# New instruction orders for four engines, and two constants written by GpSimd, in a fused attention and gMLP kernel

## The chip, the cores and the metric

The kernel runs on one core of a Trainium2 chip. The metric is the device time of one execution in microseconds (us); the figure for a kernel is the median of its runs. The engines are called by the names of the profile: PE is TensorE (matmuls), PEld is its weight load, DVE is VectorE, ACT is ScalarE, POOL is GpSimd, SP is SyncE, which here issues most DMAs.

## The reference

Tokens S = 2048, width D = 448, 16 heads of 28, gMLP half width Fh = 896, all bf16. Each token attends to itself and to the 7 tokens at distances 2, 4, ... 14 before it.

```python
# A: sliding, dilated attention on layernorm(x)
qkv = layernorm(x) @ wqkv                      # 16 heads, Dh = 28
idx = pos[:, None] - 2 * arange(8)[None, :]    # mask idx >= 0
attn = softmax(einsum(q, k[idx]) * Dh ** -0.5)
h = x + einsum(attn, v[idx]) @ wo
# B: gMLP on layernorm(h)
z = gelu(layernorm(h) @ w_in)                  # S x 1792
z1, z2 = z[:, :896], layernorm(z[:, 896:])
g = w_sp @ z2 + b_sp[:, None]                  # S x S times S x 896
h2 = h + (z1 * g) @ w_out
```

## The kernel before

The work is cut into 677 tasks, each of one engine, each with a name. A function adds them with the tasks they depend on and the buffers they take and free. The order in which each engine issues its tasks is written out by hand: `SEQ` holds five lists of task numbers, for SP, GpSimd, VectorE, ScalarE and TensorE. A planner (`Planner.replay`) goes through the lists at build time with estimated durations, picks buffers for each task (the eight PSUM banks above all, mostly in pairs), and calls the tasks' emit functions. From the order of emission `Sched` works out which semaphore each instruction waits for. So the lists, and the banks that the planner picks along them, are all that decides the order; nothing is decided at run time.

The stages, with the task names that follow later and their lines in the profile:

- Start: 16 x blocks of 128 tokens are loaded (`x`), and the weights. `c_...` tasks write constants: `c_warm` (128x512 ones, line 614), `c_wo0` (zeros in the padded output weights, 128x896 float32, line 627), `c_wkp` and `c_wqp` (625), `c_V` (628), `c_ident` (618), `c_nhalf` (616). `f0` (635) is 15 matmuls on `warm` that nobody reads; they run before the first real work.
- Layer norm 1, by units of two blocks: `bn1` (statistics, 656 and 657), `rs1` (one over the deviation, on GpSimd at 646 and 647 or on ScalarE at 668 and 669), `nrm1` (676), and a transpose into `xh`, either by a transposing DMA from SP (`tD1`, 683) or on TensorE (`tT1`, 692, with a copy `ev1`).
- Projections: `cpq` and `cpk` copy weights into a padded layout (`cpq100` is the part for one half of the heads). `mmq`, `mmk` (783) and `mmv` (823) are matmuls into a pair of banks, `evq`, `evk` and `evv` copy the banks out, on ScalarE (641) or VectorE (643). `mmk0` needs the units 0 to 3 of `xh`.
- Attention, in 9 blocks of 114 queries, from the last to the first: `mml` (logits, 858), `exp` (870), `mask` (877), `mmr` (sums over keys, 8 matmuls, 886), `ln` and `rex` (899 and 921, the inverse of the sums on ScalarE), `mmo` (values, 911), `ot` (product, 929). Then `mmy` (output projection, 964) and `h` (add to x, 972). `cpw` copies halves of `w_in`.
- Layer norm 2 (`bn2`, `rs2`, `nrm2`, `tD2`), like the first.
- gelu stage: `mmz2` (984) and `mmz1` (1028), groups of 14 matmuls into a pair of banks, emptied by `ge` (994) and `gz1` (1038) on ScalarE; layer norm 3 on the second half (`bn3` at 1000, `ag3` at 1006, `rs3`, `nrm3` at 1014).
- Gating: `g` (1064) multiplies with `w_sp`, 16 matmuls a group, 28 groups; `ua` and `um` (1073) add the bias and multiply. Then `wo` (1093), `oa` (1103) and the stores. `w_sp` arrives by transposing DMAs (`wsp`, 946), each issued when one before it has landed.

An engine issues strictly in list order: if a task waits, all that stands behind it in that list waits too. A task that takes banks waits until the task that empties them has ended.

Of the kernel before, what the change touches and what calls it, by code (L numbers as in the profile page):

```python
# [6 lines left out]
D = 448  # L7
# [21 lines left out]
F32 = mybir.dt.float32  # L29
# [191 lines left out]
class Planner:  # L221
# [12 lines left out]
    def add(self, *a, **k):  # L234
        t = Task(*a, **k)
        self.tasks.append(t)
        self.named[t.name] = t
        return t
# [140 lines left out]
def bass_sequential_preLN__sliding_local_dilated__mixer_gmlp__prompt_kernel(  # L379
# [18 lines left out]
    with contextlib.ExitStack() as top:  # L398
        def sb(name, shape, dt):
            return top.enter_context(nc.sbuf_tensor(name, shape, dt))  # L400
# [14 lines left out]
        reg3 = sb("reg3", [128, n3], BF16)  # L415
# [5 lines left out]
        warm = sb("warm", [128, 512], BF16)  # L421
# [51 lines left out]
        r_wo = [Res("wo%d" % h) for h in range(4)]  # L473
# [20 lines left out]
        r_warm = Res("warm")  # L494
# [113 lines left out]
        def cst(name, fns, dur, eng="pool", deps=()):  # L608
            def em():
                for fn, rd, wr in fns:  # L610
                    iss(eng, fn, reads=rd, writes=wr)
            return add(name, eng, dur, em, deps=deps)

        c_warm = cst("c_warm", [(lambda e: e.memset(warm[:], 1.0), [], [r_warm])], 0.5, eng="dve")
        c_eps = cst("c_eps", [(lambda e: e.memset(epst[:], EPS), [], [r_eps])], 0.1)
        c_nhalf = cst("c_nhalf", [(lambda e: e.memset(nhalf[:], -0.5), [], [r_nhalf])], 0.1)
        c_ident = cst("c_ident", [
# [6 lines left out]
        for p in "kq":  # L624
            c_wp[p] = cst("c_w%sp" % p, [(lambda e, t=wpd[p]: e.memset(t.rearrange("p c (h d) -> p (c h) d", d=32)[:, :, DH:32], 0.0),
                                          [], r_w[p][0] + r_w[p][1])], 0.5)
        c_wo0 = cst("c_wo0", [(lambda e: e.memset(reg3[:, 0:4 * D].bitcast(F32), 0.0), [], r_wo)], 1.0, eng="dve")
        c_V = cst("c_V", [(lambda e, v=v: e.memset(V[:, v, :, :, DH:32], 0.0), [], [r_V[v]]) for v in range(NV)], 0.75)

        def fill(name, n, deps=()):  # L630
# [134 lines left out]
        for ch in range(NCH - 1, -1, -1):  # L765
            for isq in (0, 1):
# [6 lines left out]
                for g0 in range(0, 4, per):  # L773
# [33 lines left out]
                   eng="dve", deps=t_k[NCH - 1] + [c_kpad])  # L807
# [356 lines left out]
```

## Time and profile before

| | us |
|---|---|
| median of 3 runs | 242.24 (242.14 to 242.91) |
| profiled execution | 242.4 |
| its span | 240.7 |
| TensorE busy | 232.7 (97%) |
| VectorE busy | 141.2 (59%) |
| ScalarE busy | 93.6 (39%) |
| GpSimd busy | 26.2 (11%) |

The profile is one execution, seen by instructions. "Busy" leaves out waits and DMA issues. The span runs from the first to the last instruction, and the execution's own time is 1.7 us longer. TensorE works through projections and attention until about 80 us, through the gelu stage until about 119 us, and through gating and output after that.

In the rows of the timeline the columns are start, duration, engine, line, operation, output and input, shape and count; a bracket holds the idle time of that engine just before and what ended it. In the DMA view, queue 8 ("instruction") carries packets of program code.

### The profile page before, as it was taken

To read this page: it belongs to the slowest core of one execution; us is meant where nothing else is said; L and a number is where in the kernel's file an instruction comes from. 1 tells how busy PE (TensorE), PEld (TensorE's weight loads), DVE (VectorE), ACT (ScalarE), POOL (GpSimd) and SP (SyncE) were. 2 spreads that over 40 slices of the span, in tenths; PEclk is the share of its full clock that TensorE was granted. 3 is DMA by queue.
4 is the path that set the end of the run, shared out by engine and by line. 5 is a ranking of instruction groups with operands and counts; after the bars stand their busy time and mean duration, and the time that the engine had idled before them with its cause. 6 is when DMAs were issued, how large, how long until landed. Compare 5 with 4: busy or idle time off the path is not lost.

```text
span 240.7 us, 6694 instructions
## 1 busy us (share of the span) xinstructions
PE 232.7 (97%) x3009; PEld 119.7 (50%) x3019; DVE 141.2 (59%) x281; ACT 93.6 (39%) x112; POOL 26.2 (11%) x66
## 2 busy tenths in 40 slices
PE   7899999999999999999999999999999999999994
PEld 2587755455545444444444444444444444444452
DVE  6999957588998999788800040271201454654443
ACT  2997988888999557664710000000000000000000
POOL 4062000002023313106400000000000000000000
PEclk9999999999999999999999999999999999999999
DMA  7924699331224378979346333200000000010122
GB/s 213 337 51 101 125 146 209 81 71 36 41 41 87 82 116 221 138 168 133 87 87 134 87 87 87 46 0 0 0 0 3 0 0 19 22 59 1 56 76 78
DMA packets 54629, 20.01 MB, mean 83 GB/s; under 512 B 46792, under 2 KB 54472, under 8 KB 54600
## 3 DMA queue, kind: packets, MB, share of 16 engines
q1 hardware_dynamic: 53416, 18.61, 36.0%
q10 hardware_dynamic: 1184, 0.98, 1.5%
q8 instruction: 23, 0.38, 0.6%
q14 instruction: 6, 0.05, 0.1%
HBM read 6.37 MB, written 1.84 MB: 34 GB/s over the span
## 4 chain that ended last, share of the span: by engine, by line
PE 88%; DVE 5%; ACT 1%; issue 1%; DMA 1%; POOL 1%
PE psum L1064 40%; PE psum L783 11%; PE psum L1093 9%; PE psum L984 8%; PE psum L964 5%; PE psum L823 5%; PE psum L1028 4%; PE psum L858 2%; PE psum L911 2%; DVE z2p L1014 2%; DMA x_tm<-in_A_x_dram 1%; PE psum L886 1%; DVE st L1000 1%; DVE st L656 1%; POOL rs L647 1%
## 5 line engine op out<-in xcount | busy, mean ns | idle before, releaser
L1073 DVE TENSOR_TENSOR ub<-psum,reg 128x512 bf16<-128x512 f32 x28 | 18.9, 687 | 68.7 <-PE psum L1064 66.4
L1064 PE MATMUL psum<-reg,z2p 128*128 128x512 bf16 x220 | 49.4, 379 | 0.2
L1064 PE MATMUL psum<-wspT_lo,z2p 128*128 128x512 bf16 x218 | 48.5, 379 | 0.4 <-DVE z2p L1014 0.2
L1064 PEld LDWEIGHTS psum<-wspT_lo,z2p 128*128 128x128 bf16 x224 | 21.8, 98 | 26.6 <-issue 0.4
L1064 PEld LDWEIGHTS psum<-reg,z2p 128*128 128x128 bf16 x224 | 21.9, 98 | 26.2
L783 PE MATMUL psum<-xh,reg 64*128 64x128 bf16 (+2 forms) x448 | 26.1, 270 | 0.1
L1093 PE MATMUL psum<-reg 128*128 128x448 bf16 (+2 forms) x119 | 22.2, 341 | 0.1
L984 PE MATMUL psum<-w_in,xh 64*128 64x448 bf16 x224 | 22.2, 349 | 0.0
L1028 PE MATMUL psum<-xh,w_in 64*128 64x512 bf16 x196 | 21.8, 376 | 0.0
L641 ACT ACTIVATE reg<-psum 128x896 bf16<-128x896 f32 (+2 forms) x25 | 19.9, 847 | 2.2 <-PE psum L823 1.2
L783 PEld LDWEIGHTS psum<-xh,reg 64*128 64x128 bf16 x448 | 16.7, 94 | 7.8 <-issue 0.6
L656 DVE BATCH_NORM_STATS2 st<-x_tm 128x6 f32<-128x448 bf16 x32 | 19.6, 611 | 1.0 <-DMA x_tm<-in_A_x_dram 0.9
L1000 DVE BATCH_NORM_STATS2 st<-z2p 128x6 f32<-128x448 bf16 x32 | 17.5, 610 | 3.6 <-ACT z2p L994 3.6
L870 ACT ACTIVATE reg<-psum 128x928 bf16<-128x928 f32 x18 | 16.2, 939 | 3.0 <-PE psum L858 3.0
L994 ACT ACTIVATE z2p<-psum 128x896 bf16<-128x896 f32 x16 | 14.2, 916 | 7.9 <-PE psum L984 7.9
L1038 ACT ACTIVATE reg<-psum 128x1024 bf16<-128x1024 f32 x14 | 13.6, 1029 | 8.0 <-PE psum L1028 8.0
L1093 PEld LDWEIGHTS psum<-reg 128*128 128x128 bf16 x119 | 11.4, 98 | 10.4
L646 POOL TENSOR_SCALAR rs<-mv 128x2 f32<-128x2 f32 x19 | 6.6, 347 | 87.9 <-DVE mv L657 69.1
L1103 DVE TENSOR_TENSOR tring<-psum,x_tm 128x448 bf16<-128x448 f32 (+2 forms) x17 | 10.1, 596 | 10.2 <-PE psum L1093 10.1
L984 PEld LDWEIGHTS psum<-w_in,xh 64*128 64x128 bf16 x224 | 10.6, 94 | 10.4 <-issue 0.4
L1028 PEld LDWEIGHTS psum<-xh,w_in 64*128 64x128 bf16 x196 | 9.4, 94 | 11.5 <-issue 0.2
L647 POOL TENSOR_TENSOR rs<-rs,nhalf 128x2 f32<-128x2 f32 x19 | 14.6, 770 | 1.6
(62 smaller groups left out, 200.7 us busy)
## 6 DMA issues: line engine op xcount, KB each, us to landing
x_tm<-in_A_x_dram SPq DMA_DIRECT2D x15, 112.0 KB, 4.0
out_dram<-tring SPq DMA_DIRECT2D x15, 112.0 KB, 1.7
w_in<-in_B_w_in_dram SPq DMA_DIRECT2D x2, 448.0 KB, 4.0
reg<-in_B_w_out_dram SPq DMA_DIRECT2D x1, 784.0 KB, 5.2
z2p<-in_A_wqkv_dram ACTq DMA_DIRECT2D x2, 336.0 KB, 4.3
reg<-in_B_b_sp_dram SPq DMA_DIRECT2D x1, 512.0 KB, 4.8
w_in<-in_B_w_in_dram SPq DMA_DIRECT2D x2, 224.0 KB, 3.4
reg<-in_A_wo_dram SPq DMA_DIRECT2D x4, 98.0 KB
```

The lines of the kernel that those rows point to most:

```text
L641: iss("act", lambda e: e.activation(dst, src, AF.Copy), reads=rd, writes=wr)
L647: iss("pool", lambda e: e.tensor_tensor(dst, dst, nh, ALU.pow), reads=rr + [r_nhalf], writes=rr)
L656: iss("dve", lambda e: e.bn_stats(st[:, b, :], x_tm[:, b, :]), reads=[r_x[b]], writes=[rl[b]])
L783: iss("pe", lambda e, c=c, s=s, gi=gi, lhs=lhs: e.matmul(psum[:, bk[s] * 512 + cw * gi:bk[s] * 512 + cw * gi + cw], lhs, xh[64 * s:64 * s ...
L870: iss("act", lambda e: e.activation(E[:, es[0], 2 * n:2 * n + 2, :], pair_view(lb, 0, 8 * JW), AF.Exp, scale=SCALE), reads=[r_bank[lb[0]], ...
L984: iss("pe", lambda e, k2=k2, c=BLK[s][k2], s=s: e.matmul(psum[:, zb[s] * 512:zb[s] * 512 + D], xh[64 * s:64 * s + 64, c, HX + 128 * u:HX + ...
L994: iss("act", lambda e: e.activation(z2p[:, u:u + 9:8, D * k:D * k + D], pair_view(zb, 0, D), AF.Gelu_apprx_tanh), reads=[r_bank[zb[0]], r_ ...
L1000: iss("dve", lambda e, b=b: e.bn_stats(st3[:, b, k, :], z2p[:, b, D * k:D * k + D]), reads=[r_z2[b][k]], writes=[r_st3[b][k]])
L1028: iss("pe", lambda e, k=k, c=BLK[s][k], s=s: e.matmul(psum[:, bk[s] * 512:bk[s] * 512 + 512], w_in[64 * s:64 * s + 64, k, 128 * f:128 * f ...
L1064: iss("pe", lambda e, b=b: e.matmul(psum[:, gb[0] * 512:gb[0] * 512 + 512], z2p[:, b, 128 * f:128 * f + 128], src[:, b, 512 * (tc % 2):512 ...
L1073: iss("dve", lambda e: e.tensor_tensor(ub[:, us_[0], :], psum[:, gb[0] * 512:gb[0] * 512 + 512], bb[:, 512 * tc:512 * tc + 512], ALU.add), ...
L1093: iss("pe", lambda e, f=f: e.matmul(psum[:, wb[0] * 512 + d0:wb[0] * 512 + d1], z1p[f][:, 128 * m:128 * m + 128], w_out[:, f, d0:d1], star ...
```

## The change

No task is added, removed or resized. Two constants change engine, and the lists of GpSimd, VectorE, ScalarE and TensorE are new; SP's list is the same. From the second gating task on (TensorE) and from `ua1_4` on (VectorE) the orders agree with those before, except that `g0_4_0` and `g1_1_0` swap.

What moves, by names:

- GpSimd: `c_warm` first, then `c_wqp`, `c_ident`, `c_wkp`, `c_V`, `c_eps`, `c_xpad`, `c_nhalf`, `c_wo0`; `c_mband` behind `rs1_5` and `c_kpad`; `rs2_0` ahead of `rs3_7`, `rs3_3` ahead of `rs3_4`.
- VectorE: no longer `c_warm` and `c_wo0`; `cpq100` from behind `nrm1_12` to right behind `cpv0`; `mask7` ahead of `nrm1_3`; `evq0_2` leaves for ScalarE, `evq0_3` (ahead of `ot5`) and `evk0_3` (behind `cpw1_0`, ahead of `h7`) come from there; `cpw1_0` behind `cpw1_1`; `nrm2_15` ahead of `h5`, `h2` ahead of `nrm2_5`; `bn3_7_0` ahead of `nrm2_2`, and many small moves among `bn3`, `ag3` and `nrm3`, whose last is now `nrm3_3` instead of `nrm3_1`.
- ScalarE: `cpk001`, `evq3_0`, `evv8` ahead of `cpq101`; `evk3_2` ahead of `cpq110`; `exp8_0` ahead of `exp7_0`; `rs1_2` ahead of `evv6`; `evq1_0` ahead of `exp7_1`; `exp5_0` ahead of `exp6_0`; `evq0_2` behind `exp6_0`; `ln5` ahead of `evk0_1`; `gz1_1_4` ahead of `ge6_1`; `ge6_0` from behind `ge6_1` to behind `ge3_1`; `ge1_1` ahead of `gz1_0_6`, and a few more.
- TensorE: `mmk3_0` two places earlier; `mml6_00` and `mml6_11` one place earlier; `mmr5` ahead of `mmq0_3`; `mmr6` ahead of `mmo5_1`; `mmo3_3` ahead of `mmr2`; some `mmz1` groups earlier among the `mmz2` groups; `g0_4_0` ahead of `g1_1_0`.

```diff
 SEQ = (
     ...
-    (28, 31, 26, 24, 29, 27, 25, 55, 87, 48, 85, 73, 86, 330, 384, 366, 348, 402, 420, 438, 341, 456, 395, 359, 413, 467,
-     431, 377, 449),
+    (23, 29, 26, 28, 31, 24, 27, 25, 30, 55, 48, 85, 87, 73, 86, 330, 384, 366, 348, 402, 420, 438, 456, 341, 413, 395, 359,
+     467, 431, 377, 449),
     ...
-        c_warm = cst("c_warm", [(lambda e: e.memset(warm[:], 1.0), [], [r_warm])], 0.5, eng="dve")
+        c_warm = cst("c_warm", [(lambda e: e.memset(warm[:], 1.0), [], [r_warm])], 0.5)
     ...
-        c_wo0 = cst("c_wo0", [(lambda e: e.memset(reg3[:, 0:4 * D].bitcast(F32), 0.0), [], r_wo)], 1.0, eng="dve")
+        c_wo0 = cst("c_wo0", [(lambda e: e.memset(reg3[:, 0:4 * D].bitcast(F32), 0.0), [], r_wo)], 1.0)
```

The list shown is GpSimd's; the other three are changed in the same way, and `cst` without an engine means GpSimd.

34 rows, old and new, of the table SEQ are left out of this document.

## The prediction

> **What bounds the kernel now.** I read the page first, then the chain of waits in order of time, then the timeline wherever TensorE shows a gap, and the DMA view in narrow windows around those gaps. "PE" is TensorE, "SP" is SyncE.
>
> ```profile
> span 240.7 us, 6694 instructions
> PE 232.7 (97%) x3009; PEld 119.7 (50%) x3019; DVE 141.2 (59%) x281; ACT 93.6 (39%) x112; POOL 26.2 (11%) x66
> PE 88%; DVE 5%; ACT 1%; issue 1%; DMA 1%; POOL 1%
> ```
>
> The first row is the span, the second the busy shares, the third the chain that ended last. TensorE is busy for 97% and carries 88% of the chain. The change removes no matmul, so it can only win where TensorE stands still, and from the gating groups at 119 us to the end TensorE's list is the same but for two neighbouring groups that swap. So I look for TensorE's gaps before 119 us. There are four that matter.
>
> ```profile
> 7.43 0.56 PE L692 MATMUL psum<-ident,tring 128*128 128x128 bf16 x7 [0.33 <-DVE tring L676]
> 17.21 1.59 PEld L783 LDWEIGHTS psum<-xh,reg 64*128 64x128 bf16 x56 [0.18 <-DVE reg L643]
> 50.41 0.70 PE L858 MATMUL psum<-reg 32*64 32x58 bf16 x64
> 51.68 1.52 PE L823 MATMUL psum<-reg,xh 64*64 64x448 bf16 x28 [0.56 <-issue]
> 71.69 1.69 PE L964 MATMUL psum<-reg 128*128 128x448 bf16 x8 [0.58 <-DVE mv L657]
> ```
>
> The bracket is idle time and its releaser. The first gap is the start-up chain; the second waits for a weight copy on VectorE; the third has no releaser ("issue"); the fourth names VectorE, but the VectorE step it names (layer-norm statistics) is none that these matmuls read. Gaps three and four, at 51 and 71 us, I read as the arrival of code for TensorE:
>
> ```profile
> q8 instruction: 23, 0.38, 0.6%
> GB/s 0 0 410 0 0 0 0 0 0 0 0 0 0 0 0 0 0 0 0 0 0 0 0 0 0 0 0 0 0 0 0 0 0 0 0 0 0 0 0 0
> q8 instruction: 1, 0.02, 5.8%
> q8 instruction: 1, 0.02, 5.6%
> 46.75 0.93 ACT L899 ACTIVATE reg<-psum 128x928 f32<-128x928 f32 x1
> 67.98 0.39 PE L886 MATMUL psum<-reg,ones 64*32 64x464 bf16 x8
> ```
>
> Queue 8 brings 23 packets of 0.38 MB / 23 = 16 KB. The GB/s row and the row under it are the DMA view of 48.7 to 50.3 us: one packet, in the third of 40 slices, so at 48.8 us. The third q8 row is 69.0 to 70.1 us: one packet, near 69.1. Both come about 1.1 us after an event that let TensorE's instruction stream go on: `ln6` on ScalarE ended at 46.75 + 0.93 = 47.7 and freed the banks of `mmy7`; `mmr1` began at 67.98. TensorE went on 2.9 us (51.68) and 2.6 us (71.69) after the packet. So where a bank wait holds the stream, the next 16 KB are asked for late, and TensorE stops some 4 us later. The gap at 51 us costs 0.56 idle by its row, and 0.06 more, since a group can start that much ahead of the modelled end of the one before it (60.44 against 60.11 + 0.39, below): some 0.62 us.
>
> **The change part by part.**
>
> Constants. GpSimd starts its own work at 0.78, VectorE at 0.96:
>
> ```profile
> 0.78 0.47 POOL L625 MEMSET reg<- 128x448 bf16 x1 [0.29 <-POOLq L1149]
> 0.96 0.48 DVE L614 MEMSET warm<- 128x512 bf16 x1 [0.96 <-PEq L1149]
> 2.10 0.20 POOL L618 MEMSET ident<- 128x128 bf16 x1
> 3.81 0.10 POOL L616 MEMSET nhalf<- 128x2 f32 x1
> 6.20 0.36 DVE L676 TENSOR_SCALAR tring<-x_tm,mv,rs 128x448 bf16<-128x448 bf16 x1
> 9.66 0.85 SPq L936 DMA_DIRECT2D reg<-in_A_wo_dram  x2
> ```
>
> GpSimd took 0.20 us for 128 elements and 0.47 for 448, so 0.83 ns an element: `c_warm` (512) about 0.53 us, `c_wo0` (896) about 0.85 by elements, up to 1.7 if its 4-byte elements count twice. The warm-up matmuls start some 0.15 us earlier. That buys nothing: what follows them waits until 7.43 for the layer-norm chain, whose list on VectorE is unchanged. GpSimd's list ended at 3.91; with both it ends near 5.5 (6.3 at the upper end) and its first user, the output-weight loads, is issued at 9.66. Cover is ample: cost 0. VectorE gains nothing either, it was waiting for the first x rows. A rule speaks against this part: the Trainium skill, SBUF — State Buffer, in its opening part on the two sides, says that VectorE's two-port modes and GpSimd lock a port pair from each other for a whole instruction. By that rule a late `c_wo0` could hold up the step at 6.20; at 0.85 us it is over by then, and no row here shows such a hold.
>
> The copies at 9 to 17 us. `cpq100` leaves the place that made the 0.18 us wait. But ScalarE now takes a bank copy (`evk3_2`, 0.5 to 0.6 us) ahead of `cpq110`, which the same matmuls need:
>
> ```profile
> 15.54 0.95 ACT L641 ACTIVATE reg<-z2p 64x896 bf16<-64x896 bf16 x1
> ```
>
> `cpq110` ended at 16.49; with 0.6 more it ends near 17.1, and `mmq3_2` starts at about 17.17 instead of 17.21. I take 0, with 0.2 of gain as the other end.
>
> Layer-norm 1, 20 to 33 us. ScalarE's `rs1_2` moves ahead of `evv6`, `exp8_0` ahead of `exp7_0`:
>
> ```profile
> 22.15 0.59 DVE L656 BATCH_NORM_STATS2 st<-x_tm 128x6 f32<-128x448 bf16 x1
> 22.70 0.29 ACT L668 ACTIVATE rs<-mv,epst 128x2 f32<-128x2 f32 x1
> 23.13 0.28 ACT L668 ACTIVATE rs<-mv,epst 128x2 f32<-128x2 f32 x1
> 23.61 0.98 DVE L676 TENSOR_SCALAR tring<-x_tm,mv,rs 128x448 bf16<-128x448 bf16 x3
> 28.42 1.22 SPq L683 DMA_TRANSPOSE xh<-tring  x1
> xh<-tring SPq DMA_TRANSPOSE x1, 4.6
> 33.17 0.60 PE L783 MATMUL psum<-xh,reg 64*128 64x512 bf16 x4
> ```
>
> `rs1_2` must wait for statistics that end as the 22.15 row begins, near 22.2, and behind it stand `evv6` and `rs1_0`. `rs1_0` then starts near 23.5 instead of 23.13, so `nrm1_0`, the second of the three at 23.61, slips by about 0.16 us, and with it VectorE's list up to `nrm1_11` and the transposed loads on SP. The last of these, issued at 28.42, took 4.6 us to land: 33.02, and `mmk0_0`, its user, began at 33.17. No slack: cost 0.15 (from 0 to 0.25).
>
> 35 to 50 us. `evq0_2` goes to ScalarE, `evq0_3` and `evk0_3` to VectorE (1.22 us each, as its cast of that shape at 29.35), `ln5` ahead of `evk0_1`, and `mmr5` ahead of `mmq0_3`. TensorE then leaves its projection matmuls for 8 column-sum matmuls and comes back:
>
> ```profile
> 29.35 1.22 DVE L643 CAST reg<-psum 128x1024 bf16<-128x1024 f32 x1
> 60.11 0.39 PE L886 MATMUL psum<-reg,ones 64*32 64x464 bf16 x8
> 60.44 1.69 PE L964 MATMUL psum<-reg 128*128 128x448 bf16 x8
> 42.47 1.02 ACT L641 ACTIVATE reg<-psum 128x1024 bf16<-128x1024 f32 x1 [0.49 <-PE psum L783]
> 43.98 1.02 ACT L641 ACTIVATE reg<-psum 128x1024 bf16<-128x1024 f32 x1 [0.49 <-PE psum L783]
> 46.94 1.24 DVE L929 TENSOR_TENSOR reg<-psum,reg 128x912 bf16<-128x912 f32 x1 [2.37 <-ACT reg L921]
> 48.21 1.09 DVE L643 COPY w_in<-w_in 64x3584 bf16<-64x3584 bf16 x1
> 49.91 1.09 DVE L972 TENSOR_TENSOR x_tm<-psum,x_tm 128x896 bf16<-128x896 f32 x1 [0.61 <-PE psum L964]
> ```
>
> The 8 take 0.33 us between their neighbours at 60 us, and about 0.2 in company of their own kind: an extra in-and-out costs some 0.2 us (0 to 0.3). In return `ln5` no longer stands behind `evk0_1` and `evq0_3` (42.47 and 43.98): `mmk0_1` ends at 42.4, `mmr5` 0.35 later, and from 42.8 ScalarE does `ln5` (0.93), `evk0_1` (1.02), `rex5` (0.98) and `ln6` (0.93), so that `rex5` ends near 45.7 and `ln6` near 46.6 instead of 47.7. Then `mmy7` is not held, the packet is asked for about 1.1 us earlier, and comes near 47.7 instead of 48.8. A transposed weight load is in flight then; it may hold the packet for part of its stay, but over a microsecond of room is left. The gap of 0.62 us goes: that is the change's gain. The Trainium skill, Runtime: NRT & Kernel Launch, section Instruction fetch mechanics, has code refilled in 16 KiB blocks and the crossing "mostly hidden". The packet size agrees; by that rule there is no gap to win here and the sum would be 242.6; the two gaps behind late packets speak against it.
>
> What is late next: VectorE. Its idle 2.37 us before `ot5` and 0.61 before `h7` are filled. From 45.7 come `ot5` 1.24, two copies of 1.09, `evk0_3` 1.22, `h7` 1.09, less 0.08 of overlap at each seam: `h7` ends near 51.4 instead of 51.0. `mmv4` takes `h7`'s banks, so TensorE goes on at about 51.5, some 0.1 later than its own work would allow.
>
> After that I find no cost. At 62 us `mmo3_3` and `mmr2` swap and push `ln2` by 0.1 us, under ScalarE's cover. In the gelu stage `ge6_0` holds two banks some 10 us longer, but each ScalarE copy (1.03 us at most) fits the 1.32 to 1.55 us that TensorE spends on a group of 14 matmuls (2.65 us from 86.12 to 88.77 for two, 6.21 for four):
>
> ```profile
> L1038 ACT ACTIVATE reg<-psum 128x1024 bf16<-128x1024 f32 x14 | 13.6, 1029 | 8.0 <-PE psum L1028 8.0
> 86.12 2.81 PE L984 MATMUL psum<-w_in,xh 64*128 64x448 bf16 x28
> 88.77 6.21 PE L1028 MATMUL psum<-xh,w_in 64*128 64x512 bf16 x56
> ```
>
> ScalarE waits for TensorE there, not the reverse. The reordered `bn3`, `ag3` and `nrm3` end near 120 us as now, and the swapped gating groups need the last of them 2 us after they start.
>
> Sum: +0.15 +0.2 -0.62 +0.1 = about -0.16 us. The profiled execution took 242.4 (span 240.7 and 1.7 around it), 0.16 over the median of 242.24. So 242.24 in the profile's terms, and 242.1 for the median.
>
> **The rivals.**
>
> Faster. The transposed loads do not slip, the wait at 17 us goes (0.18) and the switch costs nothing: -0.62 - 0.18 and 0.1 of the gap at 71 us, 241.3. More of that gap is not to be had: `ot0` and `mmy0` are tied to ScalarE behind it.
>
> ```profile
> 78.93 0.38 PEld L964 LDWEIGHTS psum<-reg 128*128 128x128 bf16 x3 [0.19 <-DVE reg L929]
> ```
>
> For it: the slips I find are 0.1 to 0.2 us, at the limit of reading. Against: TensorE, already waiting there, gives back what it wins.
>
> Not what it says. The packet is held by the transposed load until 48.8 as now, or the gap is not code: +0.15 +0.2, 242.6 in the profile's terms, 242.4 in the median's.
>
> Slower: VectorE becomes the bound at 50 to 53 us. If `mmv4`'s banks are those of `ot6`, behind `h7`, or VectorE runs later than I add up, TensorE stands until `ot6` ends, 1.2 us on: it resumes near 52.65 instead of 51.68, +0.97, 243.2. It decides once VectorE is over 0.2 us later than my sum. For it: 1.2 us net is moved to VectorE, and its idle time there is all spent. Against: `mask4` and `h6` have slack right behind.
>
> **How the numbers follow.** A measurement of this kernel can tell about 0.3%, 0.73 us: faster is below 241.51, slower above 242.97. Forecast 0.36, "not what it says" 0.12 (both within), faster 0.22, slower 0.30: a late packet elsewhere belongs to the last two, since each moves 0.6 us or more. The range reaches from just under the faster case to just over the slower one, 241.1 to 243.4.
>
> **What would show it.** Right: the 16 KB packet of 48.8 lies near 47.7, no "issue" gap ahead of L823 near 51, `ln6` ends near 46.6, L823 starts near 51.5; the gap at 71 us stays. Wrong: that gap is as wide as before, VectorE's L929 releases L823, L783 near 33.2 starts over 0.3 later, or TensorE waits for ScalarE between 86 and 119 us.

## The result, and the profile after

The kernel before took 242.40 us (median of 19 runs, 241.84 to 243.19), the changed kernel 241.27 us (median of 19, 240.85 to 242.86): a ratio of 0.9951, 95% interval 0.9939 to 0.9964. It is faster by 0.5%, some 1.1 us. The first profiled run of the changed kernel was the slowest of its 19, so the profile shown here is that of a second profiled run of the same kernel, e1_after below (240.91 us, the fastest of 6 there, whose median was 241.52; the ratio was 0.9952, 0.9937 to 0.9968).

Its page: the span, the busy times, and the shares of the chain that ended last.

```profile
span 239.1 us, 6691 instructions
PE 232.1 (97%) x3009; PEld 119.2 (50%) x3019; DVE 141.1 (59%) x280; ACT 92.5 (39%) x111; POOL 27.4 (11%) x68
PE 84%; DVE 5%; ACT 4%; POOL 3%; issue 2%; DMA 2%; POOLq 1%; SPq 0%
```

The span is 1.5 us shorter than in the profile before. The timeline at the places that the prediction named:

```profile
7.55 0.56 PE L692 MATMUL psum<-ident,tring 128*128 128x128 bf16 x7 [1.44 <-DVE tring L676]
51.09 1.52 PE L823 MATMUL psum<-reg,xh 64*64 64x448 bf16 x28 [0.18 <-DVE x_tm L972]
70.76 1.69 PE L964 MATMUL psum<-reg 128*128 128x448 bf16 x8
```

The "issue" gap of 0.56 us ahead of L823 is gone and VectorE's L972 releases it instead, with 0.18 us; the gap of 0.58 us ahead of L964 near 71 us is gone too in this run. (Three later runs with the same lists from 34 us on, e5, e6 and e12 below, still have it, with 0.40 to 0.64 us.) But all that is worth 0.58 us by the end: TensorE's last matmul starts at 236.36 instead of 236.94 (the last starts in the two traces). The other 0.95 us lies behind TensorE, in a place that the prediction never asked about. VectorE's last two output steps and the stores behind them, first in the kernel before (timeline, then the DMA view from 237.0 to 240.7 us), then in the changed kernel (236.5 to 239.2 us):

```profile
236.77 0.74 DVE L1103 TENSOR_TENSOR tring<-psum,x_tm 128x304 bf16<-128x304 f32 x2 [0.28 <-PE psum L1093]
DMA  0001799500006971067500000000000000000000
q14 instruction: 1, 0.01, 0.6%
out_dram<-tring SPq DMA_DIRECT2D x1, 76.0 KB, 1.6
out_dram<-tring SPq DMA_DIRECT2D x1, 36.0 KB, 2.5
```

```profile
236.19 0.74 DVE L1103 TENSOR_TENSOR tring<-psum,x_tm 128x304 bf16<-128x304 f32 x2 [0.28 <-PE psum L1093]
DMA  0000699993000004998300497200000000000000
out_dram<-tring SPq DMA_DIRECT2D x1, 76.0 KB, 1.6
out_dram<-tring SPq DMA_DIRECT2D x1, 36.0 KB, 1.6
```

Before, VectorE ends at 236.77 + 0.74 = 237.51 and the span 3.16 us later; after, 236.93 and 2.21 us. The last store, 36 KB, takes 2.5 us to land before and 1.6 after. In the window of before there is one instruction packet on queue 14 (8 KB, at 238.84, as the trace dates it), in the middle of that store; in the window of after there is none. In the changed kernel this packet comes at 240.30, when the program is over. In its first profiled run the end was as short: 2.20 us behind VectorE's last step.

### The profile page after: what moved, and what is told of

Same layout as the page of the kernel before. It is cut to its first block, busy times and chain, and to the rows that moved or that the text cites. A ratio compares the mean times of both kernels' runs of the same rounds, so it can differ in the third digit from the quotient of the medians.

```text
span 241.1 us, 6691 instructions
## 1 busy us (share of the span) xinstructions
PE 234.0 (97%) x3009; PEld 119.8 (50%) x3019; DVE 141.3 (59%) x280; ACT 92.9 (39%) x111; POOL 27.1 (11%) x68
## 3 DMA queue, kind: packets, MB, share of 16 engines
HBM read 6.37 MB, written 1.84 MB: 34 GB/s over the span
## 4 chain that ended last, share of the span: by engine, by line
PE 85%; DVE 5%; POOL 3%; issue 2%; DMA 2%; ACT 1%; POOLq 1%; ACTq 0%
PE psum L1064 40%; PE psum L783 9%; PE psum L1093 9%; PE psum L984 8%; PE psum L823 5%; PE psum L964 5%; PE psum L1028 4%; PE psum L858 2%; DMA z2p<-in_A_wqkv_dram 2%; POOL rs L647 2%; PE psum L911 1%; DVE x_tm L972 1%; DVE w_in L643 1%; DVE reg L643 1%; PE psum L886 1%
## 5 line engine op out<-in xcount | busy, mean ns | idle before, releaser
L783 PE MATMUL psum<-xh,reg 64*128 64x128 bf16 (+2 forms) x448 | 26.4, 270 | 0.4 <-issue 0.4
L984 PE MATMUL psum<-w_in,xh 64*128 64x448 bf16 x224 | 22.4, 349 | 0.0
L783 PEld LDWEIGHTS psum<-xh,reg 64*128 64x128 bf16 x448 | 16.8, 94 | 7.9 <-issue 1.4
L641 ACT ACTIVATE reg<-psum 128x896 bf16<-128x896 f32 (+2 forms) x24 | 19.4, 838 | 1.1 <-PE psum L783 0.9
L870 ACT ACTIVATE reg<-psum 128x928 bf16<-128x928 f32 x18 | 16.3, 944 | 5.2 <-PE psum L858 5.2
L984 PEld LDWEIGHTS psum<-w_in,xh 64*128 64x128 bf16 x224 | 10.6, 94 | 10.5 <-issue 0.4
```

Of the source, the lines that this page charges most:

```text
L641: iss("act", lambda e: e.activation(dst, src, AF.Copy), reads=rd, writes=wr)
L783: iss("pe", lambda e, c=c, s=s, gi=gi, lhs=lhs: e.matmul(psum[:, bk[s] * 512 + cw * gi:bk[s] * 512 + cw * gi + cw], lhs, xh[64 * s:64 * s ...
L870: iss("act", lambda e: e.activation(E[:, es[0], 2 * n:2 * n + 2, :], pair_view(lb, 0, 8 * JW), AF.Exp, scale=SCALE), reads=[r_bank[lb[0]], ...
L984: iss("pe", lambda e, k2=k2, c=BLK[s][k2], s=s: e.matmul(psum[:, zb[s] * 512:zb[s] * 512 + D], xh[64 * s:64 * s + 64, c, HX + 128 * u:HX + ...
```

## The experiments

All ratios are against the kernel before on the same chip, with the 95% interval. "Records" are VectorE's instructions in the trace, waits that stand alone included; "packet" is the last 8 KB packet of queue 14 against the end of VectorE's last step; "end piece" is from there to the end of the span; "matmul" is the start of TensorE's last matmul against the kernel before (236.94).

| kernel | records | packet us | end piece us | matmul us | ratio |
|---|---|---|---|---|---|
| before | 320 | +1.33 | 3.16 | 0 | 1 |
| changed (e1_after) | 318 | +3.36 | 2.21 | -0.58 | 0.9952 (0.9937 to 0.9968) |
| e2_start | 318 | +3.35 | 2.21 | +1.15 | 0.9951 (0.9934 to 0.9968) |
| e3_mid | 321 | +0.41 | 2.46 | -0.01 | 0.9961 (0.9946 to 0.9975) |
| e4_late | 319 | +3.30 | 2.21 | +0.26 | 0.9963 (0.9951 to 0.9975) |
| e5_after_v3 | 321 | +0.72 | 2.77 | -0.15 | 0.9955 (0.9924 to 0.9986) |
| e6_after_v2 | 320 | +1.23 | 3.10 | -0.37 | 0.9971 (0.9952 to 0.9991) |
| e7_before_wo0 | 319 | +3.29 | 2.21 | +0.08 | 0.9947 (0.9927 to 0.9967) |
| e8_before_v12 | 332 | -5.83 | 2.21 | +0.17 | 0.9946 (0.9928 to 0.9965) |
| e9_after_pe20 | 318 | +3.15 | 2.01 | +0.68 | 0.9984 (0.9963 to 1.0004) |
| e10_before_pe20 | 320 | +1.50 | 3.32 | +1.33 | 1.0031 (1.0009 to 1.0053) |
| e11_before_wo0_pe20 | 319 | +3.30 | 2.21 | -0.13 | 0.9990 (0.9970 to 1.0009) |
| e12_start_of_before | 318 | +3.35 | 2.21 | -0.07 | 0.9955 (0.9938 to 0.9972) |

### The change in three parts

The changed kernel once more, and the kernel before with one stretch of the changed lists each. The main moves of the middle stretch, by the tasks' names (VectorE's and some swaps of neighbours are left out):

```diff
 ScalarE, behind evk0_0
-exp6_0 exp5_0 exp5_1 exp6_1 evq0_0 evk0_1 evq0_3 ln5 rex5 ln6 evq0_1 evk0_3 rex6 exp4_0 exp4_1
+exp5_0 exp6_0 evq0_2 exp5_1 exp6_1 evq0_0 ln5 evk0_1 rex5 ln6 evq0_1 rex6 exp4_1 exp4_0
 TensorE, behind mmk0_1
-mmq0_3 mmr5 mmo5_0 mmo5_1 mmr6
+mmr5 mmq0_3 mmo5_0 mmr6 mmo5_1
```

> The changed kernel once more, for a profile of a usual run (the profiled run on record, 242.86 us, was the slowest of its 19; their median was 241.27). All theories: 241.2 us, 1.1 under the kernel before. Theory 1 (the gap at 51 us): its trace has the 16 KB packet of 48.8 us about 1 us earlier relative to TensorE's work, the gap before L823 near 51 smaller by 0.3 to 0.6 us, and the start up to 33 us within 0.2 us of before. Theory 2 (the start): TensorE reaches L783's group at 33 us already 0.6 to 1.1 us earlier than before, and the gap at 51 is nearly as wide as it was. Theory 3 (late): the two traces lie within 0.3 us of each other up to 60 us, and the rest is won at the gap of 71 us or in the gelu stage.

> The kernel before with only the first part of the change: the two constants on GpSimd and all four lists as changed up to the start of mmk0_2 at about 34 us; from there on the lists of before. Theory 1: +0.15 us (the slipped layer-norm steps), 242.4 to 242.6. Theory 2: it carries the gain, -0.6 to -1.1 us, 241.2 to 241.7. Theory 3: 0, 242.3. If the parts depend on each other (the code packets are one chain), it gives between 0 and -0.6 and the three parts do not add up.

> The kernel before with only the middle part of the change, the lists from mmk0_2 at 34 us to mmv4 at 52 us: mmr5 ahead of mmq0_3, ln5 ahead of evk0_1, evq0_2 on ScalarE, evq0_3 and evk0_3 on VectorE, and the neighbouring swaps. Theory 1: it carries the gain at the gap of 51 us, -0.3 to -0.6 us, 241.7 to 242.0, with the 16 KB packet near 47.7 us. Theory 2: +0.1 to +0.2 (the extra switch), 242.4 to 242.5. Theory 3: 0.

> The kernel before with only the last part of the change, the lists from 52 us on (mmo3_3 ahead of mmr2, h and nrm2 swaps, the gelu stage, rs3, ag3, nrm3, the gating swap). Theories 1 and 2: 0 within 0.2 us, 242.2 to 242.5. Theory 3: -0.5 to -1.1 us, 241.2 to 241.8, with the gap of 71 us smaller by about 0.5 or a wait gone after 80 us.

Medians: 241.52, 241.73, 241.95 and 241.86 us against 242.87 before. Each third of the change alone wins about as much as the whole, and none of the three theories allows that. The late part is the plainest: its lists are those of before up to 52 us, TensorE ends 0.26 us later than before by the trace, and still the kernel is 1.0 us faster. What the faster kernels share is the end piece in the table. That gave a fourth theory: VectorE's code comes in 8 KB packets; in the kernel before the last of them is asked for just as the last stores go out, any edit that takes an instruction or a lone wait off VectorE's list puts that off until the program is over, and one that adds an instruction, as the middle part does, brings it sooner.

### VectorE's last code packet

Tiny memsets into a tile that nobody reads, ahead of VectorE's list (3 and 2 in the changed kernel, 12 in the kernel before); and one constant alone moved from VectorE to GpSimd in the kernel before.

```diff
-            block.vector(lambda eng: sch.emit("dve", eng))
+            block.vector(lambda eng: ([eng.memset(dum[:, 2 * i:2 * i + 2], 0.0) for i in range(3)], sch.emit("dve", eng)))
```

```diff
-        c_wo0 = cst("c_wo0", [(lambda e: e.memset(reg3[:, 0:4 * D].bitcast(F32), 0.0), [], r_wo)], 1.0, eng="dve")
+        c_wo0 = cst("c_wo0", [(lambda e: e.memset(reg3[:, 0:4 * D].bitcast(F32), 0.0), [], r_wo)], 1.0)
```

> The changed kernel with three tiny memsets (128x2, into a tile nobody reads) ahead of VectorE's list; all else equal. Code-page theory: what the change wins at the end is that VectorE's last 8 KB code packet is no longer asked for while the last stores are under way; the kernel before asks for it at 320 VectorE records in the trace (packet at 238.84, last store 2.5 us to land instead of 1.6), kernels with 319 or fewer ask for it after the end. Three more instructions put the changed kernel where the kernel before is: the packet returns among the last stores, the last store takes over 2 us, and the time rises by 0.7 to 1.0 us, to 242.3 (in this comparison, before minus 0.3). Rival (the lists themselves win the time, and the ends of the profiled runs differed by chance): 0.0 to +0.1 against the changed kernel, before minus 1.2.

> The changed kernel with two tiny memsets ahead of VectorE's list, one fewer than in the run beside it. Code-page theory: the packet still comes after the end, so no change: before minus 1.2 us, and the last store takes 1.6 us. Rival: the same. Only if more VectorE instructions cost time by themselves does it lie between.

> The kernel before with one constant alone, c_wo0, moved from VectorE to GpSimd; all four lists otherwise as before. VectorE has one instruction fewer. Code-page theory: the last packet comes after the end, the last store takes 1.6 us, before minus 0.7 to 1.0 us. Rival, and the prediction's own first step (constants cost and win nothing): 0.

> The kernel before with twelve tiny memsets ahead of VectorE's list: only work added. Code-page theory: the last packet is asked for some 12 instructions earlier, near 226 to 230 us, where a store has 1.3 us until the next one and nobody waits for it, so the end is as short as in the changed kernel and the time falls by 0.7 to 1.0 us although work was added. Rival: 0 to +0.7 (twelve memsets of about 0.06 us at the start).

Medians: 241.65, 242.15, 241.74 and 241.79 us against 242.80 before. One instruction fewer on VectorE wins 1.06 us with no list reordered; twelve instructions more win 1.01 us. The run with the twelve, first VectorE's last two steps with the last store (from the DMA view of 237.0 to 239.9 us), then the DMA view of 231.6 to 232.5 us:

```profile
236.94 0.74 DVE L1103 TENSOR_TENSOR tring<-psum,x_tm 128x304 bf16<-128x304 f32 x2 [0.28 <-PE psum L1093]
out_dram<-tring SPq DMA_DIRECT2D x1, 36.0 KB, 1.6
DMA  0000000000090000000000000002546989999999
q14 instruction: 1, 0.01, 3.6%
```

The packet stands by itself at 231.85 (the lone 9, in the twelfth of 40 slices of 0.0225 us), with the next store still to come, and the last store takes 1.6 us. Two earlier packets of the queue came sooner with it, at 16.48 and 90.75 us instead of 20.80 and 97.67; the others stayed within 0.4 us. So the packet is VectorE's, and harmless where no store is in flight.

The changed kernel with two memsets missed its expectation, and by its place in the table it speaks for the theory: I had put the limit between two and three memsets, but two already bring the list to 320 records, the count of the kernel before. Its last two steps, and the DMA view of 236.5 to 240.3 us:

```profile
236.40 0.74 DVE L1103 TENSOR_TENSOR tring<-psum,x_tm 128x304 bf16<-128x304 f32 x2 [0.28 <-PE psum L1093]
q14 instruction: 1, 0.01, 0.7%
out_dram<-tring SPq DMA_DIRECT2D x1, 76.0 KB, 1.6
out_dram<-tring SPq DMA_DIRECT2D x1, 36.0 KB, 2.5
```

The slow store of 2.5 us and the end piece of 3.10 us are back. With three memsets (321 records, as in the middle part of the change) the packet comes 0.5 us sooner and falls across the last two stores:

```profile
out_dram<-tring SPq DMA_DIRECT2D x1, 76.0 KB, 2.4
out_dram<-tring SPq DMA_DIRECT2D x1, 36.0 KB, 2.2
```

That costs 0.56 us in the end piece (2.77 against 2.21), less than the 0.7 to 1.0 I expected. In whole times these two are less sharp than in the traces: their intervals are 0.4 to 0.6% wide and do not exclude the changed kernel's ratio. Nor did the run with two memsets fall back to the kernel before: its end piece is all but the same (3.10 against 3.16), yet it is 0.65 us faster, with an interval that excludes 1. So the rest of the change seems to win something besides, 0.2 to 1.2 us by that interval; its trace shows 0.37 of it at TensorE's last matmul. In every kernel with 320 records or more, VectorE had begun 318 or 319 of them 1 us before the packet.

### TensorE's code packets

20 matmuls of 8 columns behind the warm-up, where TensorE stands idle anyway; no result uses them. They put every later TensorE instruction 40 places on (a weight load and a matmul each).

```diff
-                for _ in range(n):
-                    iss("pe", lambda e: e.matmul(psum[:, fb[0] * 512:fb[0] * 512 + 512], warm[:, 0:128], warm[:, :]),
+                for j in range(n + 20):
+                    iss("pe", lambda e, w=512 if j < n else 8: e.matmul(psum[:, fb[0] * 512:fb[0] * 512 + w], warm[:, 0:128], warm[:, 0:w]),
```

> The changed kernel with 20 tiny matmuls (128x128 weights, 8 columns) behind the 15 warm-up matmuls, where TensorE stands idle for 1.4 us: work added that no result uses; it puts every later TensorE instruction 40 places on, so that the 16 KB code packets are asked for 40 instructions earlier in the work. Code reading of the gaps at 51 and 71 us: the packet of about 48.3 us is then asked for ahead of the bank waits of mmy7 and comes before 47 us, and the one of 68.4 about 0.4 to 1 us earlier; both gaps (0.37 and 0.5 us in the changed kernel) go, 0.4 to 0.9 us less than the changed kernel, so before minus 1.6 to 2.1, unless a packet comes late at a new place. Rival (the gaps are waits for other engines, as the rows' releasers name for the one at 71 us): 0 to +0.2 against the changed kernel, the gaps stay.

> The kernel before with the same 20 tiny matmuls. Code reading: the gaps of 0.62 us at 51 us and 0.58 at 71 us go, before minus 0.6 to 1.2 us, with none of the change in it; VectorE's last packet still falls among the last stores (3.1 us from VectorE's last step to the end of the span). Rival: 0 to +0.2.

> The kernel before with c_wo0 on GpSimd (one VectorE instruction fewer) and the 20 tiny matmuls; all lists otherwise as before. If both code readings hold they add up: -1.0 for VectorE's last packet and -0.6 to -1.2 for TensorE's two, before minus 1.6 to 2.2 us, which is 0.4 to 1.0 under the changed kernel. Rival (TensorE's gaps are no code): before minus 1.0.

Medians: 242.57, 243.89 and 242.88 us against 242.85. The mechanism held, the price had the wrong sign. The timeline of the kernel before with the 20 matmuls:

```profile
23.52 1.70 PE L783 MATMUL psum<-xh,reg 64*128 64x256 bf16 x28 [0.64 <-issue]
52.59 0.35 PE L858 MATMUL psum<-reg 32*64 32x58 bf16 x20 [0.70 <-issue]
71.38 0.25 PE L858 MATMUL psum<-reg 32*64 32x58 bf16 x5 [0.33 <-issue]
```

Before, the gap at 51 us stood between L858's 64 matmuls and L823; now it stands inside L858, with 20 of the 64 to go: 20 weight loads and matmuls earlier in the work, just the 40 places. The gap at 71 us moved from ahead of L964 over the 14 matmuls of L984 and the last 5 of L858, which is 19 of the 20 (some matmul records can be missing). Its releaser changed from VectorE's statistics to "issue" with it. A wait for data would have stayed with its matmul; so both gaps are TensorE's code. But they did not go, and one of 0.64 us came up at 23 us. In the changed kernel with the 20, the packet of 48.3 us came at 46.8, as expected. But the 0.37 and 0.5 us that were to be won there did not exist: its trace without the 20 has only 0.18 us at 51 us, behind VectorE, and no gap at 71 (the rows of the section on the result). And new gaps opened:

```profile
41.13 1.90 PE L783 MATMUL psum<-xh,reg 64*128 64x512 bf16 x16 [0.37 <-issue]
59.42 1.10 PE L964 MATMUL psum<-reg 128*128 128x448 bf16 x5 [0.25 <-issue]
70.71 0.24 PE L858 MATMUL psum<-reg 32*64 32x58 bf16 x5 [0.24 <-issue]
```

By the ratios the 20 matmuls cost 0.3% to 0.4%, 0.75 to 1.05 us, in all three kernels. The profiled run of the third was the fastest of its 12 and shows no gap at 51 or 71 us; how its other runs lost a microsecond was not seen.

### The start of the lists

The last run keeps both constants on GpSimd and the changed lists from 34 us on, and takes the start from before. The main moves:

```diff
 VectorE, behind cpv0
-cpq100 bn1_12 cpk010 cpk011 bn1_4 cpk000 bn1_13 cpq111 bn1_5 nrm1_4 bn1_1 nrm1_12 nrm1_5
+bn1_12 cpk010 cpk011 bn1_4 cpk000 bn1_13 cpq111 bn1_5 nrm1_4 bn1_1 nrm1_12 cpq100 nrm1_5
 TensorE, behind mmk3_2
-mmk3_0 mmk2_2 mmk2_0
+mmk2_2 mmk2_0 mmk3_0
```

> The changed kernel with the start of its four lists (to mmk0_2, about 34 us) as in the kernel before; the two constants on GpSimd and the lists from 34 us on as changed. VectorE has 319 records, so its last packet comes after the end. If the lists' start wins what the changed kernel's trace shows there (L783 at 33 us 0.3 us earlier than before), this run lies 0.3 us above the changed kernel, before minus 0.9; if the start wins nothing that lasts, it equals the changed kernel, before minus 1.2; if the reordered start is what makes the changed kernel's slowest runs, it is a little faster and its runs lie closer together.

It took 241.56 us (241.24 to 242.12, 9 runs) against 242.66, 1.1 less: between the expectations for the time, with an interval that holds them all. VectorE has 318 records, not 319, and its packet comes after the end all the same. Its profiled run reaches L783 at 33 us 0.4 us later than the changed kernel's; whether that lasts stays open. No version tried beats the changed kernel by what a comparison can tell.

## Why the prediction was right or wrong, step by step

The time, 241.27, lies inside the range, but that was luck: 0.16 us of gain was forecast, 1.13 came, and most of it lies in none of the steps (0.95 of the 1.53 us between the two traces). The rival that came out faster, 241.3, had the time right and the reason wrong.

**The step that failed** is the first, the constants, in its sentence "VectorE gains nothing either", and behind it the premise that the change "can only win where TensorE stands still". Durations were right to 0.01 us for both memsets (GpSimd's rows in the changed kernel's timeline):

```profile
0.78 0.52 POOL L614 MEMSET warm<- 128x512 bf16 x1 [0.29 <-POOLq L1149]
4.55 0.84 POOL L627 MEMSET reg<- 128x896 f32 x1
```

Predicted were 0.53 and 0.85, with GpSimd's list ending near 5.5; it ended at 5.39, and no hold of VectorE's next step is seen. But the two instructions were costed as work and not as places in VectorE's program. Without the two, with one copy more and one lone wait fewer, VectorE's list has 318 records instead of 320, and that moved the last packet out of the last store: -0.95 us where the sum had 0. The row was there before: a 36 KB store that takes 2.5 us behind a 76 KB one that takes 1.6. The Trainium skill, Runtime: NRT & Kernel Launch, section Instruction fetch mechanics, calls the crossing of a code block "mostly hidden". In the kernel before it cost VectorE nothing and the last store 0.9 us.

**Copies, 9 to 17 us.** Cost 0, with 0.2 as the other end: the other end it was, the wait of 0.18 us at 17 us has no row in the profile of the changed kernel shown here.

**Layer-norm 1.** The slip came, and was covered. VectorE's three steps of L676 and the statistics behind them, then the last transposed load and its user, in the changed kernel (timeline; the fourth row is the DMA view's time to landing):

```profile
23.43 1.16 DVE L676 TENSOR_SCALAR tring<-x_tm,mv,rs 128x448 bf16<-128x448 bf16 x3
24.50 0.62 DVE L656 BATCH_NORM_STATS2 st<-x_tm 128x6 f32<-128x448 bf16 x1
28.43 2.19 SPq L683 DMA_TRANSPOSE xh<-tring  x1
xh<-tring SPq DMA_TRANSPOSE x1, 3.5
32.87 1.47 PE L783 MATMUL psum<-xh,reg 64*128 64x512 bf16 x12
```

The three steps took 1.16 us instead of 0.98, close to the slip of 0.16 predicted. But VectorE came to them 0.18 us earlier than before (23.43 instead of 23.61), so the statistics behind them begin at 24.50 as before, and the load was issued when it was before (28.43 against 28.42). It then landed at 31.9 and not at 33.0; why it was quicker stays open. "No slack" was a reading too strong: L783 follows TensorE's own work without a gap in both traces, and it started 0.30 us earlier, not 0.15 later.

**35 to 50 us.** This step can be read by itself in the run with the middle part alone (timeline; the GB/s row and the row under it are its DMA view of 47.7 to 49.2 us):

```profile
42.86 0.94 ACT L899 ACTIVATE reg<-psum 128x928 f32<-128x928 f32 x1 [0.53 <-PE psum L886]
45.47 0.95 ACT L899 ACTIVATE reg<-psum 128x928 f32<-128x928 f32 x1
50.28 1.09 DVE L972 TENSOR_TENSOR x_tm<-psum,x_tm 128x896 bf16<-128x896 f32 x1
51.42 1.52 PE L823 MATMUL psum<-reg,xh 64*64 64x448 bf16 x28 [0.18 <-DVE x_tm L972]
GB/s 0 0 0 0 437 0 0 55 75 89 109 143 123 143 137 109 157 109 82 143 232 212 205 259 218 164 150 130 157 123 61 34 0 0 0 0 0 0 0 0
q8 instruction: 1, 0.02, 6.2%
71.70 1.67 PE L964 MATMUL psum<-reg 128*128 128x448 bf16 x8 [0.84 <-DVE mv L657]
```

Predicted: `ln5` from 42.8 (42.86), `ln6` to 46.6 (46.42), the packet near 47.7 (47.87), `h7` to 51.4 (51.37), L823 at 51.5 behind `h7`'s banks (51.42, released by L972), in sum -0.32 us with the switch of 0.2 (51.42 against 51.68, so -0.26). The chain was right link by link. (Two sums in it are slightly off: from 45.7 its five steps end at 51.1 with the overlap it takes off and at 51.4 without, and they ran almost without; the terms of the whole add to -0.17, not -0.16.) In this run it was worth nothing in the end: the gap at 71 us, which stays, grew from 0.58 to 0.84, since its packet came only 0.2 us earlier, and took the 0.26 back. The prediction had said that TensorE, already waiting there, gives back what it wins, but only against the rival; its own sum left the gain standing.

**52 us on.** In the traces from 80 us on no kernel with the changed late lists loses anything: the distance to the kernel before is the same at 95 us and at the end, to 0.05 us.

**The rivals.** VectorE did become what L823 waits for, but for 0.18 us and not for 0.97: the slower rival's point was not reached. "Not what it says" did not come true either, the packet moved. In the faster one, the transposed loads that did not slip and the wait that went were right, and TensorE ends 0.58 us earlier in the best run. There its "more of that gap is not to be had" held too: TensorE's lead was 0.94 us behind the gap at 71 us and 0.58 at 80, and the wait of L964's weight load at 78 us for VectorE's L929 grew from 0.19 to 0.47. But the kernels that have only the short end piece (0.9947, 0.9946) are as fast as the changed one (0.9951, 0.9952). How much the new lists win by themselves is not settled: by the traces TensorE ends 0.07 to 0.58 us earlier in e1, e5, e6 and e12, and whole times show it in one run alone (e6_after_v2).

## What to carry to other kernels

Before giving any edit a price, look behind the last compute instruction: how long the last store takes beside the one ahead of it, and whether an instruction packet lies in it. Cost an added or removed instruction, and a lone wait, twice: as work, and as a place in its engine's program that moves every later code packet of that engine. If several unrelated parts of a change each win the whole gain, they share a side effect; compare the traces where their edits are not.

## What the runs showed that I had not expected

VectorE's code comes in packets of 8 KB, TensorE's in packets of 16 KB (8,192 and 16,384 bytes in the traces). One of 8 KB among the last stores holds the end for 0.25 to 1.1 us by its place (end pieces of 2.46 to 3.32 us against 2.21). Half of the 0.95 us in the kernel before is the data: the last data packet ends 1.84 us behind VectorE's last step instead of 1.34. The other half lies between that packet and SyncE's going on (0.86 instead of 0.40 us); what it is made of stays open.

The changed start also has a bad form. In the first profiled run of the changed kernel, and in that of its start alone, TensorE lost 0.9 to 1.4 us near 20 us (the first row is the former, the second the latter):

```profile
21.32 0.71 PE L858 MATMUL psum<-reg 32*64 32x58 bf16 x64 [0.71 <-issue]
20.86 0.71 PE L858 MATMUL psum<-reg 32*64 32x58 bf16 x64 [1.21 <-ACT reg L870]
```

Both stand at the same matmul, and in the second profiled run of the changed kernel there is no gap there. In the first, another gap, of 0.37 us, stands at 17.11. A late code packet would fit: TensorE's packets came at 18.56 and 17.98 us there, 2.8 and 2.9 us before it went on, as at 51 us before the change, and at 16.34 in the run without the gap. ScalarE's L870, which the second row names, can hardly be the cause, since TensorE passed that matmul in the run without the gap before L870's first step (19.74 us, 0.9 long) had ended. No experiment tried it.
